# Gated attention and MLP on one core: one weight load moved ahead of two attention loads, its splits ahead of an evacuation

## The chip, the cores and the metric

The kernel runs on 1 core of one Trainium2 chip. The metric is the device time of one execution in microseconds, the median over several runs; lower is better. The work is spread over the core's engines: TensorE (PE in the profile, its weight loads PEld), VectorE (DVE), ScalarE (ACT), GpSimd (POOL), and SyncE (SP), which here issues every DMA.

## What is computed

For a sequence of 2048 tokens of width D = 448 the kernel computes two branches on the same x and mixes them by a gate of one number per token:

```python
x = A_x
g = _sigmoid((x * gate_w).sum(-1, keepdims=True))
# branch A: 16 heads of 28; each token attends to 8 positions, every second one back from itself
qkv = x @ wqkv
logits = einsum("bhsd,bhswd->bhsw", q, kg) * scale      # masked where the position is below 0
a = (softmax(logits) applied to vg) @ wo
# branch B: F = 1792
h = relu(x @ w1 + b1) ** 2
b = h @ w2 + b2
return g * a + (1 - g) * b
```

All inputs and the output are float32. Each product is made of three passes over a high and a low part of both operands (high·high, high·low, low·high), so every operand is first split: a copy that rounds to the high part, and a subtraction that leaves the low part.

## The kernel before

**Stages.** Tokens come in four chunks of 512 (chunk order in the MLP: 3, 0, 1, 2). First TensorE makes q, k and v of chunks 0, 1 and 2; ScalarE copies the results out of PSUM (the evacuations, L243) into staging tiles, and SP stores these to DRAM (`q_d`, `k_d`, `v_d`). Then comes chunk 3 in two calls of `qkv_two`, two token tiles each. The second call has the first two pairs of MLP hidden tiles (`mlp_one`, `mlp_two`) put in between its own products. After that comes the MLP for all chunks, `h` products (x by w1) and `b` products (h by w2) in turn, with the output projection `a` worked in near the end.

**Attention** runs beside all this on GpSimd and VectorE, in eight units: GpSimd multiplies q by k (L561, eight pieces of a unit), VectorE sums the products (L562), then softmax, then GpSimd multiplies by v (L568). A unit's q and k are loaded by SP (L532 and L533) into one buffer each, so the loads for the second unit wait until GpSimd has finished the first unit's eight pieces.

**What sets the order.** Nothing is scheduled at run time: each engine runs its instructions in the order in which the Python code emits them. A model clock, `clock["pe"]`, is moved on by `advance` with each group of matmuls; `when(t, fn, ...)` and `at(dt, fn)` put a piece of work on a list, and `advance` emits what is due. So the numbers in the `when` table decide where in an engine's queue a piece stands; they are not times on the chip. If a piece waits for data, everything behind it on that engine waits too.

**The weights w2.** `w2_piece(i0, n, t, gap)` loads n row blocks of w2 (128x448 each) into one buffer of the two-buffer pool `rawp` (L792) and puts one split per block at t, t + gap and so on. The first load holds blocks 0 to 3 (896 KB), the second blocks 4 to 6 (672 KB). A split (`split_copied`) is a ScalarE copy to the high part `w2ah` (L745), a second ScalarE copy of the raw block into one PSUM bank, `copy` (L746), and a VectorE subtraction to the low part `w2al` (L751). All seven splits share the one `copy` bank, so a second copy waits for the subtraction before it. The first load's buffer is the one that the third w1 load had: its last readers are ScalarE's copies of that load.

**PSUM banks.** There are eight, four of tag "m" and four of tag "b". In the second `qkv_two` the accumulators q0, q1 and k1 hold three "m" banks, and the first hidden pair (h0, h1) takes the fourth and then q0's bank, once ScalarE has evacuated q0. A hidden pair's products come in two halves, between which the two tiles change sides of the array; ScalarE marks the change by a touch of the weights (L814, `h_turn`), which waits for the first half and for which the second half waits. In the same way a VectorE memset (L212, `turned` and `turn`) marks the change for q, k and v.

**The biases.** `biases()` issues two DMAs: b1 into `b1t` (part of tile `b1z`, L1024), used by the ReLU on ScalarE (L867), and b2 spread over all partitions into `b2t` (L1025). Until then `b2t` serves as the staging tile of a v evacuation, whose store is the DMA `v_d<-b2t` (L230).

Of the kernel before, what the change touches and what calls it, by code (L numbers as in the profile page):

```python
# [57 lines left out]
def gated_mix_kernel(ctx: ExitStack, tc: tile.TileContext, xT, wqkv, w1, w2, wo, b1, b2, out):  # L58
# [868 lines left out]
    def when(t, fn, *args):  # L927
        later.append((t, lambda: fn(*args)))
# [129 lines left out]
    when(66000.0, w1_piece, 3, 83700.0, 900.0)  # L1058
    for j in range(2):
        when(63700.0 + j * 2000.0, x_copy, 3, j)  # L1060
    when(76700.0, biases)
    when(83700.0, w2_piece, 0, 4, 93400.0, 1350.0)
    when(87400.0, w2_piece, 4, 3, 99000.0, 1350.0)

    pair = {}
# [441 lines left out]
```

## Time and profile before

| | us |
|---|---|
| median of 3 runs | 413.45 (413.06 to 413.98) |
| the profiled execution: time, and its span | 414.4, 412.6 |
| PE busy in the span | 405.5 (98%) |
| DVE, ACT, POOL busy | 288.2, 219.3, 267.4 |
| PE idle in the stretch 100 to 115 | 2.22 of 15 |
| granted TensorE clock | 1.0 |

The profile shows one execution, which took 0.95 us more than the median; its span leaves out 1.8 us of that execution's time. Busy time is a sum over stages; what a change of order is worth is read from the stage in which it stands, from what each engine waited for there. In rows of a timeline the first number is the start and the second the duration, both in us from the span's start, and a bracket at the end gives the idle time of the engine just before that row and what ended it.

### The profile page before, as it was taken

The page shows a single profiled execution, that of the slowest core. Times are in us where ns is not written, and L with a number is a line of the kernel's source. Part 1 is how long each engine was busy: PE and PEld are TensorE (multiplying, and loading weights), DVE is VectorE, ACT ScalarE, POOL GpSimd, SP SyncE. Part 2 cuts the span into 40 slices and gives each one's busy share as a digit, 9 for nine tenths or more (in the row PEclk, how much of TensorE's full clock was granted, in tenths as well). Part 3 has the DMA queues.
Part 4 walks back from the last instruction along what each step waited for, and adds up shares of the span by engine and source line. Part 5 has one row for each costly group of instructions (what it writes and reads, how often), then busy time and mean ns, then how long its engine had stood idle before and what let it go on. Part 6 is the DMA issues. An engine that isn't in the chain of part 4 may idle for free.

```text
span 412.6 us, 9369 instructions
## 1 busy us (share of the span) xinstructions
PE 405.5 (98%) x3799; PEld 361.8 (88%) x3799; DVE 288.2 (70%) x480; ACT 219.3 (53%) x498; POOL 267.4 (65%) x167
## 2 busy tenths in 40 slices
PE   8999999999999999999999999999999999999996
PEld 7999999998878888888888888988898888888996
DVE  3997884674768667687755898779676677784344
ACT  4858577372875565444565435444643254346640
POOL 0000001864999999979999799898989978950000
PEclk9999999999999999999999999999999999999999
DMA  7999999949463605654023648855146630049404
GB/s 217 353 359 262 361 374 259 371 132 348 166 210 127 207 4 179 207 186 152 8 78 106 193 140 247 248 153 157 39 153 197 220 129 0 25 126 180 120 3 178
DMA packets 67548, 73.99 MB, mean 179 GB/s; under 512 B 34544, under 2 KB 59824, under 8 KB 67376
## 3 DMA queue, kind: packets, MB, share of 16 engines
q1 hardware_dynamic: 67504, 73.39, 56.1%
q8 instruction: 29, 0.48, 0.5%
q14 instruction: 15, 0.12, 0.1%
HBM read 45.94 MB, written 28.25 MB: 180 GB/s over the span
## 4 chain that ended last, share of the span: by engine, by line
PE 92%; DMA 3%; ACT 2%; DVE 1%; issue 0%; SPq 0%
PE b L202 33%; PE h L202 31%; PE a L202 7%; PE qkv L202 7%; PE v L344 4%; PE x L344 3%; DMA w2raw<-w 2%; PE z L344 2%; PE qkv L291 2%; PE y L344 1%; PE w L344 1%; DMA xraw<-xT 1%; PE a L1279 1%; ACT st L243 1%; ACT copy L746 1%; DVE w2al L751 1%
## 5 line engine op out<-in xcount | busy, mean ns | idle before, releaser
L561 POOL TENSOR_TENSOR qk<-q,k 128x896 f32<-128x896 f32 x64 | 134.6, 2138 | 86.6 <-DMA k<-k_d 79.0
L568 POOL TENSOR_TENSOR av<-lg,v 128x896 f32<-128x896 f32 x64 | 118.9, 1976 | 4.7 <-DVE lg L562 4.5
L866 DVE TENSOR_TENSOR h<-h,h 128x512 fp32r<-128x512 f32 x56 | 38.5, 688 | 58.2 <-ACT h L869 57.7
L562 DVE TENSOR_REDUCE lg<-qk 128x32 f32<-128x896 f32 x64 | 67.1, 1074 | 0.0
L576 DVE TENSOR_REDUCE o<-av 128x112 f32<-128x896 f32 x64 | 66.6, 1070 | 0.3 <-POOL av L568 0.3
L202 PE MATMUL b<-w2ah,h 64*128 64x448 f32 x448 | 66.3, 359 | 0.0
L202 PE MATMUL b<-w2bh,h 64*128 64x448 f32 x448 | 66.1, 359 | 0.0
L867 ACT ACTIVATE h<-h,b1z 128x512 f32<-128x512 f32 x56 | 36.7, 655 | 42.1 <-PE h L202 42.1
L202 PEld LDWEIGHTS b<-w2bh,h 64*128 64x128 f32 x448 | 42.1, 184 | 3.6
L202 PEld LDWEIGHTS b<-w2ah,h 64*128 64x128 f32 x448 | 42.0, 184 | 3.7
L202 PE MATMUL b<-w2bl,h 64*128 64x448 f32 x224 | 40.6, 358 | 0.0
L202 PE MATMUL b<-w2al,h 64*128 64x448 f32 x224 | 40.5, 358 | 0.0
L202 PE MATMUL qkv<-wqh,x 64*128 64x448 f32 (+1 forms) x240 | 36.6, 361 | 0.0
L868 ACT ACTIVATE h<-h 128x512 fp32r<-128x512 f32 x56 | 33.5, 598 | 1.7
L869 ACT ACTIVATE h<-h 128x512 f32<-128x512 f32 x56 | 33.3, 594 | 0.0
L814 ACT ACTIVATE h<-h 128x4 fp32r<-128x4 f32 (+1 forms) x35 | 7.2, 207 | 43.4 <-PE b L202 41.1
L202 PEld LDWEIGHTS qkv<-wqh,x 64*128 64x128 f32 x240 | 23.7, 185 | 1.7
L202 PE MATMUL qkv<-wql,x 64*128 64x448 f32 (+1 forms) x120 | 22.8, 361 | 0.0
L202 PEld LDWEIGHTS b<-w2bl,h 64*128 64x128 f32 x224 | 21.1, 184 | 1.9
L202 PEld LDWEIGHTS b<-w2al,h 64*128 64x128 f32 x224 | 21.0, 184 | 1.9
L202 PE MATMUL h<-x,w1ah 64*128 64x512 f32 x84 | 17.4, 389 | 0.7 <-ACT w1ah L814 0.7
L243 ACT ACTIVATE st<-qkv 128x448 f32<-128x448 f32 x24 | 12.3, 542 | 7.4 <-DVE xraw L969 3.2
(280 smaller groups left out, 899.2 us busy)
## 6 DMA issues: line engine op xcount, KB each, us to landing
k<-k_d SPq DMA_DIRECT2D x8, 840.0 KB, 6.6
v<-v_d SPq DMA_DIRECT2D x8, 840.0 KB, 4.7
x_d<-x SPq DMA_DIRECT2D x12, 512.0 KB, 8.2
q_d<-st SPq DMA_DIRECT2D x8, 448.0 KB, 7.0
k_d<-st SPq DMA_DIRECT2D x8, 448.0 KB, 7.9
w1raw<-w SPq DMA_DIRECT2D x4, 896.0 KB, 14.1
q<-q_d SPq DMA_DIRECT2D x8, 448.0 KB, 4.1
o_d<-o SPq DMA_DIRECT2D x16, 224.0 KB, 2.2
```

What stands on the lines that cost most here:

```text
L202: nc.tensor.matmul(acc.pt[:, :acc.n], a[rows], w[rows], start=acc.todo == acc.all, stop=acc.todo == 1)
L243: nc.scalar.activation(st[:, :, t % 2], heads(pt), AF.Copy)
L291: nc.tensor.matmul(acc.pt[:, :D], a, w, start=k == j == 0, stop=False)
L344: nc.tensor.matmul(self.pt[:, :self.n], a, w, start=new, stop=True, skip_group_check=True)
L561: nc.gpsimd.tensor_mul(pr, q[:, s:s + 1].to_broadcast([P, W, C]), k[:, s:s + W])
L562: pending.append(lambda: nc.vector.tensor_reduce(lg[:, s], pr.rearrange("p w (h d) -> p w h d", h=HG), axis=AX.X, op=ALU.add))
L568: nc.gpsimd.tensor_mul(pr.rearrange("p (h d) w -> p w h d", h=HG), lg[:, s][:, :, :, None].to_broadcast([P, W, HG, DH]), v[:, s:s + W].rea ...
L576: nc.vector.tensor_reduce(o[:, g * C:(g + 1) * C], pr, axis=AX.X, op=ALU.add)
L866: nc.vector.tensor_sub(hl, pt, f32(hh))
L867: ops += [lambda pt=pt, r=r: nc.scalar.activation(pt, pt, AF.Relu, bias=b1t[:, f + r:f + r + 1]), lambda pt=pt, hh=hh: nc.scalar.activatio ...
L868: lambda pt=pt, hh=hh: nc.scalar.activation(hh, pt, AF.Square),
L869: lambda pt=pt, r=r, low=low: (nc.scalar.activation(pt, pt, AF.Square), at(delays[r], low))]
```

## The change

It alters three numbers and the order of two lines in the `when` table:

```diff
-    when(76700.0, biases)
-    when(83700.0, w2_piece, 0, 4, 93400.0, 1350.0)
+    when(85000.0, biases)
+    when(81000.0, w2_piece, 0, 4, 90000.0, 1350.0)
     when(87400.0, w2_piece, 4, 3, 99000.0, 1350.0)
```

No instruction is added or taken away. What moves is shown below at three places.

SP's queue, in the stretch after the last v stores of chunk 2 (`w2raw_1455` and `w2raw_1413` are the first w2 load, `w2raw_1550` the second; `q_1442` and `k_1443` are the second attention unit's; the `st` tiles are chunk 3's staged q, k and v):

```order
 L230 DMA v_d<-b2t 128x4x112
+L792 DMA w2raw_1413<-w 128x4x448
+L532 DMA q_1442<-q_d 128x896
+L533 DMA k_1443<-k_d 128x1680
+L235 DMA q_d<-st_0_0_1426 128x4x224
+L235 DMA k_d<-st_1_1_1428 128x4x224
 L1024 DMA b1z<-b 128x14
 L1025 DMA b2t<-b 128x448
-L532 DMA q_1442<-q_d 128x896
-L533 DMA k_1443<-k_d 128x1680
-L792 DMA w2raw_1455<-w 128x4x448
-L235 DMA q_d<-st_0_0_1426 128x4x224
```

The w2 load now stands first, right behind the store of `b2t`, and the two bias loads stand behind q, k and two stores.

ScalarE's queue around the evacuations of the second `qkv_two` (`qkv_2_0` is q0, `qkv_3_1` is k1), before:

```order
L243 ACTIVATE st_2_0_1618<-qkv_2_0_1490 128x4x112
L243 ACTIVATE st_3_1_1620<-qkv_3_1_1493 128x4x112
L745 ACTIVATE w2ah<-w2raw_1455 128x448
L746 ACTIVATE copy_1496<-w2raw_1455 128x448
L745 ACTIVATE w2ah<-w2raw_1455 128x448
L746 ACTIVATE copy_1496<-w2raw_1455 128x448
L814 ACTIVATE w1ah<-w1ah 128x2
```

And the same place now:

```order
L745 ACTIVATE w2ah<-w2raw_1413 128x448
L746 ACTIVATE copy_1496<-w2raw_1413 128x448
L745 ACTIVATE w2ah<-w2raw_1413 128x448
L746 ACTIVATE copy_1496<-w2raw_1413 128x448
L243 ACTIVATE st_2_0_1624<-qkv_2_0_1490 128x4x112
L243 ACTIVATE st_3_1_1626<-qkv_3_1_1493 128x4x112
L814 ACTIVATE w1ah<-w1ah 128x2
```

Two splits stand ahead of these rows in both; before, the other two of the first load came behind the evacuation of q0 and k1, and now all four come ahead of it.

VectorE's queue, the low parts against the memsets (`qkv_3_0` is k0, `qkv_2_1` is q1) and attention's sums (the change, one piece of the difference):

```order
+L751 TENSOR_TENSOR w2al<-copy_1496,w2ah 128x448
 L212 MEMSET qkv_3_0_1491 1x1
 L212 MEMSET qkv_2_1_1492 1x1
+L751 TENSOR_TENSOR w2al<-copy_1496,w2ah 128x448 x2
 L562 TENSOR_REDUCE lg_1184<-qk_7_1415 128x32
 L212 MEMSET qkv_2_2_1494 1x1
 L212 MEMSET qkv_3_2_1495 1x1
```

Three of the four low parts now stand ahead of the memsets of v and of the first unit's last sum; one of them stands ahead of the memsets of q1 and k0. The fourth comes behind the second unit's first sum.

## The prediction, made before the changed kernel was run

> **What bounds the kernel now.** I read the page's busy line first, then TensorE's own list of waits, then its windows, and went from the two waits found there to the engines behind them.
>
> ```profile
> PE 405.5 (98%) x3799; PEld 361.8 (88%) x3799; DVE 288.2 (70%) x480; ACT 219.3 (53%) x498; POOL 267.4 (65%) x167
> PE h L202 <- ACT st L243: 1.5, 1, 1.5
> PE h L202 <- ACT w1ah L814: 0.7, 1, 0.7
> 116.80:380.00 263.20, 263.20 (x2492) 232.93 (x2490) 190.69 (x247) 132.14 (x293) 231.78 (x136) 1.00 0.46 143
> ```
>
> TensorE is the bound: from 116.8 to 380 it has no idle time (the second number equals the first; the granted clock, third from the end, is 1.00). Outside the start and the end it waits for others twice, both times for ScalarE, and both waits lie in the stretch that the change rearranges. TensorE's timeline there:
>
> ```profile
> 101.81 0.39 PE L202 MATMUL h<-x,w17h 64*128 64x512 f32 x1
> 103.71 0.50 PE L202 MATMUL h<-x,w17h 64*128 64x512 f32 x1 [1.51 <-ACT st L243]
> ...
> 109.61 0.61 PE L202 MATMUL h<-x,w17h 64*128 64x512 f32 x2
> ...
> 112.33 0.36 PE L202 MATMUL qkv<-wqh,x 64*128 64x450 f32 x1
> ...
> 113.58 0.36 PE L202 MATMUL qkv<-wqh,x 64*128 64x450 f32 x1
> 114.64 0.50 PE L202 MATMUL h<-x,w1ah 64*128 64x512 f32 x2 [0.71 <-ACT w1ah L814]
> ```
>
> The idle numbers (1.51 and 0.71) understate the loss: in the first gap one half of the array had a matmul and the other none. I take the loss from the cadence. Twelve pairs of 512 columns take 2.72 (109.61 to 112.33), so nine take 2.04; six pairs of 448 or 450 columns take 1.24 (112.33 to 113.58). Undisturbed from 101.81: hidden pair 2.72, six pairs of q, k, v 1.24, second half 2.04, next hidden pair 2.72, six pairs 1.24, in all 9.96. TensorE could be at the row of 114.64 by 101.81 + 9.96 = 111.77. The two waits cost **2.87 us**, and no more than that is to be had here.
>
> ScalarE shows why:
>
> ```profile
> 86.61 0.55 ACT L746 ACTIVATE copy<-w1raw 128x448 f32<-128x448 f32 x1 [0.81 <-DVE w17l L751]
> ...
> 92.70 1.25 ACT L130 ACTIVATE w17h<-w1raw 64x64 fp32r<-64x64 f32 x4
> 100.94 0.58 ACT L745 ACTIVATE w2ah<-w2raw 128x448 fp32r<-128x448 f32 x1 [6.99 <-DMA w2raw<-w]
> 101.43 0.53 ACT L746 ACTIVATE copy<-w2raw 128x448 f32<-128x448 f32 x1
> ...
> 102.64 0.55 ACT L746 ACTIVATE copy<-w2raw 128x448 f32<-128x448 f32 x1 [0.19 <-DVE w2al L751]
> 103.13 1.07 ACT L243 ACTIVATE st<-qkv 128x448 f32<-128x448 f32 x2
> ...
> 106.75 0.21 ACT L814 ACTIVATE w1ah<-w1ah 128x2 fp32r<-128x2 f32 x1 [0.41 <-PE h L202]
> ...
> 111.83 0.64 ACT L867 ACTIVATE h<-h,b1z 128x512 f32<-128x512 f32 x1
> ...
> 114.39 0.20 ACT L814 ACTIVATE w1ah<-w1ah 128x2 fp32r<-128x2 f32 x1
> ```
>
> It stands still for 6.99 us, from the end of the w17h splits (93.95) until the first w2 load lands (100.94). Then two splits run at 1.21 us each (101.43 to 102.64), and the evacuation of q0, whose bank h1 needs, starts only at 103.13. Its data were there earlier: q0's products end six pairs before 101.81, at 100.57, plus about 0.16 (a 0.36 us matmul outlasts its 0.20 slot by that). The backlog also reaches the ReLU (111.83), and behind it the touch (114.39) that the second gap waits for. Why the load is late is on SP:
>
> ```profile
> 83.49 1.05 SPq L230 DMA_DIRECT2D v_d<-b2t  x1
> ...
> 90.06 0.35 SPq L1025 DMA_DIRECT2D b2t<-b  x1
> 90.50 0.38 SPq L532 DMA_DIRECT2D q<-q_d  x1
> 90.93 0.42 SPq L533 DMA_DIRECT2D k<-k_d  x1
> 91.45 0.39 SPq L792 DMA_DIRECT2D w2raw<-w  x1
> ...
> 97.92 1.29 SPq L792 DMA_DIRECT2D w2raw<-w  x1
> SPq L1025 <- DMA v_d<-b2t: 4.2, 1, 4.2
> 87.00:88.00 1.00, 1.00 (x14) 0.93 (x12) 1.00 (x4) 0.16 (x1) 1.00 (x2) 1.00 0.09 24
> 100.00:101.00 1.00, 1.00 (x12) 0.94 (x10) 0.00 (x0) 0.06 (x1) 1.00 (x2) 1.00 1.09 375
> 105.00:106.00 1.00, 1.00 (x12) 0.84 (x10) 0.87 (x2) 0.80 (x3) 1.00 (x2) 1.00 0.34 125
> ```
>
> The b2 load overwrites the tile that `v_d<-b2t` still reads, so SP is held for 4.2 us, to 90.06, with q, k and w2 behind it, while the DMA engines are nearly idle (0.09 busy, 24 GB/s at 87; 375 GB/s at 100).
>
> **The change part by part.**
>
> *The w2 load (one DMA) moved ahead of the biases, q and k.* It needs its buffer, which ScalarE reads last at 86.61 + 0.55 = 87.16. So it is issued at about 87.2, 4.2 us sooner. How long it then takes no row shows; the nearest, and the ones that bound it, are these landing times (the last number, from issue):
>
> ```profile
> w2raw<-w SPq DMA_DIRECT2D x1, 896.0 KB, 9.5
> k<-k_d SPq DMA_DIRECT2D x1, 840.0 KB, 7.7
> q<-q_d SPq DMA_DIRECT2D x1, 448.0 KB, 5.7
> q_d<-st SPq DMA_DIRECT2D x1, 448.0 KB, 10.4
> k<-k_d SPq DMA_DIRECT2D x1, 840.0 KB, 4.8
> w1raw<-w SPq DMA_DIRECT2D x2, 896.0 KB, 14.1
> ```
>
> The first four were issued at 90.5 to 91.9 behind one another. The k load of 4.8 is the first unit's, with little in flight; w1raw's 14.1 is of a stretch where the engines were full throughout. At 87.2 they are nearly idle, so I take the short end: 4.8 x 896/840 = 5.1, landing at 92.3 (bounds 92.3 and 101.3). ScalarE reaches the first split at 93.95, so its 6.99 us wait goes.
>
> *All four splits ahead of the q0 evacuation.* Two more are there, 2.42 us of ScalarE. Four at 1.21 from 93.95 end at 98.8, before the evacuation's data at 100.73: they lie inside the old 6.99 us of idle time and cost nothing. If the load lands after about 96, that cover is gone (rival 2). The evacuation then runs 100.73 to 101.3, before h1's slot (101.81 + 0.23). **First gap: gone.**
>
> *Low parts ahead of memsets on VectorE.*
>
> ```profile
> 96.61 0.14 DVE L212 MEMSET qkv<- 1x1 f32 x2 [1.16 <-PE qkv L202]
> 78.62 10.47 POOL L561 TENSOR_TENSOR qk<-q,k 128x896 f32<-128x896 f32 x5 [1.58 <-DMA v_d<-st]
> 98.72 6.25 POOL L561 TENSOR_TENSOR qk<-q,k 128x896 f32<-128x896 f32 x3 [9.63 <-DMA k<-k_d]
> 105.67 2.07 DVE L562 TENSOR_REDUCE lg<-qk 128x32 f32<-128x896 f32 x2
> ```
>
> The first low part is ready at about 95.5 and is over before TensorE lets the q1/k0 memsets run (96.61); these are needed at 100.57. Cost nothing, with 4 us of slack.
>
> *The q and k loads* (two DMAs) now follow the w2 load. They wait for GpSimd's last piece of the first unit (78.62 + 10.47 = 89.09) instead of SP's 90.06: issued 1.35 us sooner, with 896 KB ahead of them and the 224 KB of b2 no longer. The w2 bytes move largely in the idle time before 91, so I take a landing of 96.5 against 98.72 before. Bounds: 89.6 + 4.8 = 94.4, and 99.7 (rival 1).
>
> *The biases* (two DMAs) move past five others. Their wait is over at 90.06, before SP reaches them. b1 is first read by the ReLU, at 108.8 below; even a landing of 10.4 after an issue at 93 leaves 5 us. Behind them on SP are the v store and the second w2 load. That load was issued at 97.92 and its bytes were through before 106 (0.34 busy, then quiet); 896 KB of the traffic now leaves earlier, which at 375 GB/s is 2.4 us, so I take a landing by 103.5; its first split is due at 104.85.
>
> *The second gap.* ScalarE's chain: the touch at 104.53 + 0.19 = 104.74 (hidden pair ends 101.81 + 2.72); 0.11 to the first copy of the next split, 0.47 and 0.48 for its two copies, 0.86 for the two evacuations, 0.47, 1.21, 0.49 for the last two splits: ReLU at 108.8. From ReLU to TensorE's start took 114.64 - 111.83 = 2.81, so 111.65 against the 111.77 at which TensorE is ready. The second gap closes with 0.1 to spare, so I leave 0.1 of the 2.87 unclaimed.
>
> **Sum:** 2.8 us off TensorE's path. Behind it TensorE has no wait until 380 and the order of all engines is unaltered; the end keeps its own waits. Against the profiled execution: 414.4 - 2.8 = 411.6 (span 409.8). That execution was 0.95 above the median, so on the median 413.45 - 2.8 = 410.65, say **410.7**.
>
> **The rivals.**
>
> 1. *The keys land late, and half the gain goes.* The keys feed GpSimd; VectorE sums its products in an order in which the fifth and sixth low parts stand behind the second unit's third sum. The old landing, 98.72, puts that sum's end at 98.72 + 6.25 + 1.04 (half of 2.07) = 106.0, about when the fifth low part is wanted (105.8); each us beyond 98.8 delays the touch by as much. Counted from before: issue 1.35 sooner, 896 KB more ahead (2.4 us at 375 GB/s), would give 98.6 + 2.4 - 1.35 = 99.7: 0.9 lost, **411.6**. For it: the four landings above (96.2, 98.6, 100.9, 102.3) came in order of issue. Against it: the idle engines at 87. The Trainium skill ("DMA: Bandwidth & Descriptors", Queues, rings and completion order) says that on each DMA engine descriptors of one queue are consumed in ring order, so that what stands ahead is always paid; by that rule the time is this rival's unless the weights are through before the keys are issued. The trace's order of landing agrees.
>
> 2. *Slower: the w2 load lands late all the same.* With the splits ahead of the evacuation on an in-order engine, a late load now blocks more. Before, a landing at 100.94 let the evacuation start at 103.13, behind two splits; behind four it ends 2.19 + 2.42 + 0.54 = 5.15 after the landing X. Beyond X = 96.9 TensorE waits for it, and since the row of 114.64 follows h1's start by 9.96 - 0.23 = 9.73, it breaks even at X = 99.8. At w1raw's 14.1 from 87.2, X = 101.3: h1 at 106.45, the row of 114.64 at 116.2, time **415.0**. Against it: the full engines behind that 14.1 are absent at 87.
>
> 3. *The second w2 load lands late,* because the biases are issued ahead of it. At the old end of its bytes, 106, the chain from 104.85 moves by 1.15: **411.8**.
>
> 4. *Nothing measurable:* the load is held on SP until 91.4 by something that the trace does not show (the old row at 91.45 has no visible reason to be that late but its neighbours) and lands near 98.5, so that h1 starts about as before, and the keys behind it land near 101 and take most of the second gap back: **413.2**.
>
> **How the numbers follow.** Chances: forecast 0.70, rival 1 0.12, rival 3 0.07, rival 4 0.05, rival 2 0.06. A run of this kernel scatters from 413.06 to 413.98, so about 0.2% (0.8 us) is what can be told from no change. Forecast and rivals 1 and 3 are faster by more than that, save a rival 1 with keys later than 100.8 (0.03): faster 0.86, same 0.08, slower 0.06. The range runs from the whole 2.87 and a scatter of 0.4 (410.2) to rivals 1 and 3 with as much scatter (412.2), and leaves out 0.15.
>
> **What would show it.** Right: w2 issued near 87.2 and landed before 94, no DMA wait on ScalarE before its first w2 copy; the q0 evacuation near 100.7; TensorE without an idle row from 101 to 114, the row of 114.64 near 111.8. Wrong: a ScalarE wait on w2raw that lasts beyond 96, a VectorE wait on GpSimd's products ahead of a low part, or keys that land after 98.8.

## The result and the profile after

| | kernel before | changed kernel | changed / before |
|---|---|---|---|
| first comparison, median of 6 runs each | 413.70 us (413.06 to 414.03) | 411.34 us (411.06 to 411.82) | 0.9946, 95% 0.9933 to 0.9959 |
| repeated in a later set of runs, 20 and 8 runs | 412.53 us (411.82 to 413.36) | 411.23 us (410.9 to 412.9) | 0.9975, 95% 0.9963 to 0.9988 |
| profiled execution: time, span | 414.4, 412.6 us | 411.63, 409.9 us | |

The change makes the kernel faster, by 0.54% in the first comparison and by 0.25% in the second. 410.7 us had been predicted, with 411.6 for the profiled execution and 409.8 for its span. The changed kernel takes the same in both; what differs is the kernel before. That difference is the subject of half the experiments.

The page of the changed kernel, its busy line, followed by the shares of the engines in its chain of work:

```profile
PE 404.7 (99%) x3799; PEld 362.8 (89%) x3799; DVE 288.2 (70%) x480; ACT 219.4 (54%) x498; POOL 267.5 (65%) x167
...
PE 97%; DMA 1%; SPq 0%; DVE 0%; ACT 0%; issue 0%
```

TensorE's own waits in the changed kernel (total, times, longest), the whole list, and then two of its windows:

```profile
PE warm L879 <- DVE b1z L877: 1.2, 1, 1.2
PE qkv L291 <- ACT x L911: 0.8, 1, 0.8
100.00:115.00 15.00, 15.00 (x140) 13.99 (x140) 10.93 (x15) 10.25 (x24) 14.92 (x11) 1.00 0.30 103
115.00:380.00 265.00, 265.00 (x2510) 234.57 (x2508) 191.43 (x249) 132.37 (x295) 231.35 (x135) 1.00 0.47 143
```

Both waits for ScalarE are off the list; what is left belongs to the start. In the stretch of the change TensorE is busy for 15.00 of 15.00 us. Its timeline there, with no idle number in any row:

```profile
102.03 0.42 PE L202 MATMUL h<-x,w17h 64*128 64x512 f32 x2
...
112.02 0.42 PE L202 MATMUL h<-x,w1ah 64*128 64x512 f32 x2
...
114.10 0.37 PE L202 MATMUL b<-w2ah,h 64*128 64x448 f32 x2
```

From 102.03 to 112.02 it takes 9.99, where the prediction worked out 9.96 for an undisturbed TensorE. (This execution was 0.22 us behind the earlier one before the change bears on it: chunk 3's q, k, v start at 79.03 against 78.81. So its times are to be read 0.22 later than the predicted ones.)

SyncE of the changed kernel, then ScalarE:

```profile
83.31 1.02 SPq L230 DMA_DIRECT2D v_d<-b2t  x1
86.98 0.38 SPq L792 DMA_DIRECT2D w2raw<-w  x1
88.86 0.33 SPq L532 DMA_DIRECT2D q<-q_d  x1
89.25 0.42 SPq L533 DMA_DIRECT2D k<-k_d  x1
...
92.71 0.96 SPq L1025 DMA_DIRECT2D b2t<-b  x1
...
95.12 0.78 SPq L792 DMA_DIRECT2D w2raw<-w  x1
```

```profile
86.41 0.55 ACT L746 ACTIVATE copy<-w1raw 128x448 f32<-128x448 f32 x1 [0.80 <-DVE w17l L751]
...
92.92 1.25 ACT L130 ACTIVATE w17h<-w1raw 64x64 fp32r<-64x64 f32 x4
94.20 0.58 ACT L745 ACTIVATE w2ah<-w2raw 128x448 fp32r<-128x448 f32 x1
...
98.81 0.55 ACT L746 ACTIVATE copy<-w2raw 128x448 f32<-128x448 f32 x1 [0.19 <-DVE w2al L751]
101.36 0.98 ACT L243 ACTIVATE st<-qkv 128x448 f32<-128x448 f32 x2 [2.00 <-PE qkv L202]
...
109.10 0.64 ACT L867 ACTIVATE h<-h,b1z 128x512 f32<-128x512 f32 x1
...
111.66 0.20 ACT L814 ACTIVATE w1ah<-w1ah 128x2 fp32r<-128x2 f32 x1
```

The w2 load is issued the moment ScalarE has read its buffer (86.41 + 0.55 = 86.96), 4.5 us sooner than before. The first w2 split follows the w17h splits directly, with no wait for a DMA, and all four are over at 99.36, before the evacuation has its data. That evacuation now waits for TensorE (2.00), where TensorE used to wait for it. The last four rows end the second gap: the touch at 111.66 is over at 111.86, and the hidden row at 112.02 has nothing to wait for.

VectorE, GpSimd and the DMA engines of the changed kernel:

```profile
95.55 0.64 DVE L751 TENSOR_TENSOR w2al<-copy,w2ah 128x448 fp32r<-128x448 f32 x1
...
96.82 0.14 DVE L212 MEMSET qkv<- 1x1 f32 x2 [0.64 <-PE qkv L202]
96.36 6.31 POOL L561 TENSOR_TENSOR qk<-q,k 128x896 f32<-128x896 f32 x3 [7.53 <-DMA k<-k_d]
87.00:88.00 1.00, 1.00 (x14) 0.94 (x12) 1.00 (x5) 0.00 (x0) 1.00 (x1) 1.00 0.20 49
90.00:91.00 1.00, 1.00 (x14) 0.93 (x12) 0.41 (x1) 0.89 (x3) 0.00 (x0) 1.00 1.04 401
102.00:103.00 1.00, 1.00 (x12) 0.91 (x12) 0.61 (x2) 0.34 (x1) 1.00 (x2) 1.00 0.07 21
```

The low part stands in VectorE's idle time ahead of the memset, which still waits for TensorE. The second keys land at 96.36. The DMA engines, at 49 GB/s at 87, are at 401 GB/s at 90, three us after the issue of the weights, and by 102 nearly nothing moves any more (21 GB/s).

### The profile page after: what moved, and what is told of

Its sections match the earlier page's. It is cut to its first block, busy times and chain, and to the rows that moved or that the text cites. A ratio compares the mean times of both kernels' runs of the same rounds, so it can differ in the third digit from the quotient of the medians.

```text
span 409.9 us, 9374 instructions
## 1 busy us (share of the span) xinstructions
PE 404.7 (99%) x3799; PEld 362.8 (89%) x3799; DVE 288.2 (70%) x480; ACT 219.4 (54%) x498; POOL 267.5 (65%) x167
## 4 chain that ended last, share of the span: by engine, by line
PE 97%; DMA 1%; SPq 0%; DVE 0%; ACT 0%; issue 0%
PE b L202 33%; PE h L202 33%; PE qkv L202 11%; PE a L202 7%; PE v L344 4%; PE x L344 3%; PE z L344 2%; PE qkv L291 1%; DMA xraw<-xT 1%; PE y L344 1%; PE w L344 1%; PE a L1279 1%; PE last L1279 0%; SPq L891 0%; SPq L886 0%; DVE bt L1158 0%
## 5 line engine op out<-in xcount | busy, mean ns | idle before, releaser
L866 DVE TENSOR_TENSOR h<-h,h 128x512 fp32r<-128x512 f32 x56 | 38.5, 689 | 58.5 <-ACT h L869 58.1
L202 PEld LDWEIGHTS qkv<-wqh,x 64*128 64x128 f32 x240 | 22.8, 185 | 1.5
L202 PE MATMUL qkv<-wql,x 64*128 64x448 f32 (+1 forms) x120 | 21.9, 361 | 0.0
L202 PE MATMUL h<-x,w1ah 64*128 64x512 f32 x84 | 16.5, 387 | 0.0
```

The source lines that it names most:

```text
L202: nc.tensor.matmul(acc.pt[:, :acc.n], a[rows], w[rows], start=acc.todo == acc.all, stop=acc.todo == 1)
L866: nc.vector.tensor_sub(hl, pt, f32(hh))
```

## The experiments

**How they are read.** A few tenths of a per cent are close to the scatter of the runs, so I read each profile also by one stretch: from the start of chunk 3's q, k, v on TensorE to the first row that reads w2 (`b<-w2ah`). Undisturbed it takes 35.06, as in the second profile of the changed kernel. What it takes beyond that is what a kernel loses to waits there.

| kernel | q, k, v start | first `b` row | stretch | lost | b2 load / first w2 load issued |
|---|---|---|---|---|---|
| before, first profile | 78.81 | 116.81 | 38.00 | 2.94 | 90.06 / 91.45 |
| before, second | 78.02 | 114.24 | 36.22 | 1.16 | 87.68 / 89.07 |
| before, third | 78.39 | 114.66 | 36.27 | 1.21 | 87.38 / 89.04 |
| before, fourth | 78.67 | 114.80 | 36.13 | 1.07 | 87.34 / 88.73 |
| changed, first profile | 79.03 | 114.10 | 35.07 | 0.01 | 92.71 / 86.98 |
| changed, second | 78.69 | 113.75 | 35.06 | 0 | 92.27 / 86.59 |
| biases alone, first | 78.17 | 113.78 | 35.61 | 0.55 | 91.77 / 87.73 |
| biases alone, second | 78.59 | 114.23 | 35.64 | 0.58 | 92.05 / 88.15 |
| loads moved, old splits | 78.52 | 114.12 | 35.60 | 0.54 | 91.99 / 86.42 |
| splits alone | 78.67 | 118.20 | 39.53 | 4.47 | 87.57 / 88.96 |
| w2 and splits, old biases | 78.10 | 113.84 | 35.74 | 0.68 | 87.87 / 88.31 |
| keys behind v | 78.29 | 118.81 | 40.52 | 5.46 | 91.89 / 86.19 |
| keys last | 78.64 | 121.13 | 42.49 | 7.43 | 92.24 / 86.55 |

The first four experiments take the change apart and share one chip and one set of runs of the kernel before (412.45 us, 411.6 to 413.44, 29 runs). The recorded expectations call them e1 to e4, in this order, and the two experiments with later keys e5 and e6.

### The biases' loads alone

```diff
-    when(76700.0, biases)
+    when(85000.0, biases)
```

> Only the biases' loads are moved (w2's load stays behind q and k, two splits stay behind the evacuation of q0). Theory (only the landing time counts: the splits in the old order hold the evacuation no more once the load lands before about 98.5): q, k and w2 are issued at 89 to 90, w2 lands near 96.5, both TensorE waits are gone, 411.3 against 413.7 before, as with the whole change. Rival (the w2 load has to stand ahead of the keys): w2 lands at 98.5 or later, less than half of the gain, 412.6 or more.

Measured: 412.34 us (411.31 to 413.02, 12 runs), ratio 0.9999, 95% 0.9989 to 1.0008. That isn't the 411.3 expected. The profiled execution was the fastest of the twelve. ScalarE in it, and the row of TensorE that still waits:

```profile
97.33 0.58 ACT L745 ACTIVATE w2ah<-w2raw 128x448 fp32r<-128x448 f32 x1 [4.01 <-DMA w2raw<-w]
...
100.18 0.98 ACT L243 ACTIVATE st<-qkv 128x448 f32<-128x448 f32 x2 [0.49 <-PE qkv L202]
...
105.27 0.55 ACT L746 ACTIVATE copy<-w2raw 128x448 f32<-128x448 f32 x1 [0.45 <-DVE w2al L751]
111.61 0.50 PE L202 MATMUL h<-x,w1ah 64*128 64x512 f32 x2 [0.29 <-ACT w1ah L814]
```

The load still stands behind the keys and lands at 97.3. The evacuation is in time, so there is no first gap. But the second pair of splits comes behind the evacuation, and on VectorE the fourth low part (104.62 to 105.23) stands behind two of attention's sums: the copy of the fifth split waits 0.45 us for it, the ReLU comes later by about as much, and 0.55 us of the second gap stays. Neither the theory (both waits gone) nor its rival (w2 at 98.5 or later) describes this.

### The loads moved, the splits where they were

```diff
-    when(76700.0, biases)
-    when(83700.0, w2_piece, 0, 4, 93400.0, 1350.0)
+    when(85000.0, biases)
+    when(81000.0, w2_piece, 0, 4, 93400.0, 1350.0)
```

> Both moves of loads, but the splits where they were (two ahead of q0's evacuation, two behind). Theory: the load lands before 94, the two later splits run between the evacuation (102.3) and the touch (105.0) in ScalarE's idle time, nothing lost, 411.3. Rival (the splits' place is part of the gain, since two splits of 1.2 us stand ahead of the touch): the first gap is closed, the second is not, 412.0 to 412.5.

Measured: 411.87 us (411.45 to 413.01, 11 runs), ratio 0.9992, 95% 0.9983 to 1.0002. ScalarE and the same row of TensorE:

```profile
99.48 0.55 ACT L746 ACTIVATE copy<-w2raw 128x448 f32<-128x448 f32 x1 [4.27 <-DVE w2al L751]
100.52 0.98 ACT L243 ACTIVATE st<-qkv 128x448 f32<-128x448 f32 x2 [0.49 <-PE qkv L202]
111.94 0.50 PE L202 MATMUL h<-x,w1ah 64*128 64x512 f32 x2 [0.28 <-ACT w1ah L814]
```

No row waits for the DMA any more, yet ScalarE stands still for 4.27 us all the same: the low part that it waits for stands on VectorE behind the memsets of v, which wait for TensorE. That wait itself delays nothing, since the evacuation still has to wait for TensorE (0.49). What costs is the same wait as with the biases alone, 0.45 us of the fifth split's copy for the fourth low part: 0.54 us of the second gap stays. So the theory, that nothing is lost, fell, and the rival's account holds, though the time is below its 412.0. An early load alone isn't enough; the place of the splits in both queues is part of the gain.

### The splits alone

```diff
-    when(83700.0, w2_piece, 0, 4, 93400.0, 1350.0)
+    when(83700.0, w2_piece, 0, 4, 90000.0, 1350.0)
```

> Only the splits are moved; both loads stay as before. Theory (the prediction's rival 2: a late load behind an in-order engine): w2 lands at 100.9, the evacuation ends 5.15 later at 106.1, h1 starts there instead of at 103.7, the next half follows by 9.73 at 115.8 instead of 114.6, so slower by 1.2: 414.9. Rival (ScalarE does the same work either way, the order is neutral): 413.7.

Measured: 415.07 us (413.64 to 416.91, 6 runs), ratio 1.0062, 95% 1.0039 to 1.0085. ScalarE, TensorE, and TensorE's granted clock (third from the end) in two windows:

```profile
99.25 0.58 ACT L745 ACTIVATE w2ah<-w2raw 128x448 fp32r<-128x448 f32 x1 [5.43 <-DMA w2raw<-w]
...
103.91 0.96 ACT L243 ACTIVATE st<-qkv 128x448 f32<-128x448 f32 x2
101.05 0.47 PE L202 MATMUL qkv<-wqh,x 64*128 64x448 f32 x2 [0.42 <-DVE qkv L212]
...
104.49 0.53 PE L202 MATMUL h<-x,w17h 64*128 64x512 f32 x1 [1.73 <-ACT st L243]
104.00:106.00 2.00, 1.51 (x8) 1.29 (x10) 2.00 (x6) 0.87 (x2) 1.53 (x2) 0.71 0.03 9
106.00:108.00 2.00, 2.00 (x12) 1.56 (x12) 2.00 (x3) 0.00 (x0) 2.00 (x2) 0.50 0.00 0
```

This is the mechanism of rival 2. With four splits ahead of it the evacuation is held by a late load: the load landed at 99.25, and the evacuation's first half ends at 103.91 + 0.54 = 104.45, 5.20 later, where the prediction had 5.15. The sooner splits are a loss unless the load is early. A memset that now stands behind a low part holds TensorE too (0.42); the longer wait behind it hides that. The second hidden tile starts 2.59 late by these waits (104.49 against 78.67 + 23.23, the undisturbed distance). The rest of the 4.47 is for the most part not a wait: the granted clock falls to 0.50, which costs an estimated 1.7. It didn't fall in every execution: two of the six runs kept a clock of 1.0 and took 413.64 and 413.94, the other four, at 0.995 to 0.996, took 415.02 to 416.91. So the expected 414.9 is met by luck. The load came 1.7 sooner than expected, and the lower clock made up for it.

### The w2 load and its splits, the biases where they were

```diff
-    when(83700.0, w2_piece, 0, 4, 93400.0, 1350.0)
+    when(81000.0, w2_piece, 0, 4, 90000.0, 1350.0)
```

> w2's load and splits moved, the biases left where they were, so that SP is still held by b2 until about 90. Theory: w2 lands near 97 and the keys near 100.9; the first wait is 0.3 to 0.5, and the late keys hold the fifth and sixth low parts, so the second gap is about 2; of the gain 0.5 to 0.9 is left, 412.8 to 413.2. Rival (moving w2 ahead is the gain, the biases do not matter): 411.3.

Measured: 412.89 us (411.92 to 413.87, 12 runs), ratio 1.0009, 95% 0.9997 to 1.0021. ScalarE, GpSimd and TensorE:

```profile
95.36 0.58 ACT L745 ACTIVATE w2ah<-w2raw 128x448 fp32r<-128x448 f32 x1 [2.11 <-DMA w2raw<-w]
98.63 6.30 POOL L561 TENSOR_TENSOR qk<-q,k 128x896 f32<-128x896 f32 x3 [11.73 <-DMA k<-k_d]
111.67 0.50 PE L202 MATMUL h<-x,w1ah 64*128 64x512 f32 x2 [0.40 <-ACT w1ah L814]
```

Issued at 88.31 behind the b2 load, the weights land at 95.4, soon enough for the first gap, and the keys at 98.6. Rival 1 names 98.8 as the limit for the keys, for a first h row at 101.81; here that row is at 101.10, which puts the limit at 98.1. The keys are 0.54 late and the row of 111.67 is 0.61 late (101.10 + 9.96 = 111.06). 0.68 us of the stretch stays lost.

The time is what was expected, but not for the reasons given: the weights and the keys landed 1.6 and 2.3 us sooner than the theory says, and beside these runs of the kernel before there is no gain. Behind the stretch this profile has another wait of 0.5 that no other kernel here shows (for a hidden part of VectorE, L866). I did not follow it further.

So none of the four combinations gives a gain in its runs that can be told from no change; the whole change does. The w2 load alone, and the biases with the splits, were not run. By the profiles each of the three combinations that lose less than the kernel before still loses at least 0.5 us, and that the whole change is better than the loads without the splits rests on the profiles (0 against 0.54 lost), since the intervals of the two overlap.

### The second keys later

To test rival 1 as a rule, two kernels issue the second q and k loads of the changed kernel later, behind the v store, and behind that and the second w2 load. They differ in the delay alone (2500 and 4000):

```diff
-                if i not in qk:
+                if i not in qk and i != 1:
...
-                        qk[1] = att_load_qk(*units[1])
+                        at(2500.0, lambda: qk.update({1: att_load_qk(*units[1])}))
```

> The changed kernel with the second unit's q and k loads issued later, behind the biases and the v store, ahead of the second w2 load. Theory (rival 1's mechanism: keys that land after about 98.8 delay the touch by as much, through VectorE's sums ahead of the fifth low part): the keys land near 100.5, TensorE waits for the touch for 1.5 to 1.9, slower than the whole change by that much. Rival (attention has slack there): no wait, same time as the whole change.

> As e5, with the keys behind the second w2 load too. Theory: they land near 102.3, the wait for the touch is 3.3 to 3.7, the loss against the whole change 3.3 to 3.7, one us for each us of landing. Rival (the keys matter, but VectorE or ScalarE have slack after the first us): the loss is as in e5 or below 2.5.

These ran together with the second comparison. Behind v: 416.44 us (415.51 to 417.88, 6 runs), ratio 1.0105, 95% 1.0088 to 1.0121. Last: 418.99 us (418.76 to 419.2, 4 runs), ratio 1.0162, 95% 1.0148 to 1.0175. GpSimd, ScalarE and TensorE of the first, then GpSimd and TensorE of the second:

```profile
102.02 6.31 POOL L561 TENSOR_TENSOR qk<-q,k 128x896 f32<-128x896 f32 x3 [15.10 <-DMA k<-k_d]
110.53 0.55 ACT L746 ACTIVATE copy<-w2raw 128x448 f32<-128x448 f32 x1 [2.78 <-DVE w2al L751]
115.06 0.68 PE L202 MATMUL h<-x,w1ah 64*128 64x512 f32 x2 [3.59 <-ACT w1ah L814]
```

```profile
104.13 6.26 POOL L561 TENSOR_TENSOR qk<-q,k 128x896 f32<-128x896 f32 x3 [16.85 <-DMA k<-k_d]
117.12 0.80 PE L202 MATMUL h<-x,w1ah 64*128 64x512 f32 x2 [3.89 <-ACT w1ah L814]
```

The rule of rival 1 holds: each us of the keys beyond 98.8 delays the row behind the second gap (115.06 and 117.12 here) by as much. The first h row is at 101.29 and 101.64 in these profiles, 0.52 and 0.17 before the 101.81 on which 98.8 rests. Behind v, the row is late by 115.06 - (101.29 + 9.96) = 3.81 and the keys by 102.02 - (98.8 - 0.52) = 3.74; last, 117.12 - (101.64 + 9.96) = 5.52 and 104.13 - (98.8 - 0.17) = 5.50. The changed kernel, with its keys at 96.4, is 2.7 us on the safe side (its limit is 98.8 + 0.22). The times are 5.2 and 7.8 us above the changed kernel's, where 1.5 to 1.9 and 3.3 to 3.7 were expected, for two reasons: the keys landed 1.5 and 1.8 later than expected, and the loss is larger than the wait, because the granted clock fell in both. TensorE's windows, first behind v, then last:

```profile
114.00:116.00 2.00, 0.94 (x6) 0.76 (x8) 1.97 (x5) 2.00 (x7) 2.00 (x2) 0.80 0.00 0
116.00:118.00 2.00, 2.00 (x12) 1.63 (x10) 1.79 (x3) 1.00 (x4) 2.00 (x2) 0.50 0.06 20
```

```profile
116.00:118.00 2.00, 0.88 (x4) 0.79 (x6) 1.97 (x5) 2.00 (x7) 2.00 (x2) 0.50 0.00 0
118.00:120.00 2.00, 2.00 (x12) 1.53 (x12) 1.80 (x3) 1.05 (x5) 2.00 (x2) 0.50 0.03 10
120.00:122.00 2.00, 2.00 (x14) 1.64 (x12) 0.00 (x0) 0.63 (x1) 2.00 (x2) 0.50 1.02 307
```

### Both kernels again, and the kernel before twice more

> The whole change again, beside the kernel before on the chip of these runs, because in the runs of e1 to e4 the kernel before took 412.45 and not 413.7. Theory (what the change takes away is a loss of the kernel before that varies with the landing of the store of b2t, which held SP to 90.06 in the first profile and to 87.6 and 87.9 in e3 and e4): the changed kernel is as fast as before this, 411.0 to 411.4, and the gain is smaller here, 1.0 to 1.5. Rival (the gain is a fixed 2.4, and the whole chip was faster by 1.2): 410.0 to 410.2.

> The kernel before, profiled here. Theory: b2's load is issued at 87.6 to 88, w2 lands near 99.3, q0's evacuation ends near 102.0 and both TensorE waits together cost 1.3 to 1.8 instead of 2.9; ratio to itself 1.000. Rival (fixed loss): SP held to about 90 and TensorE waits of 1.5 and 0.7 as in the first profile.

The changed kernel: 411.23 us, ratio 0.9975 as in the table at the top. The kernel before against itself: 412.53 (411.77 to 413.72, 12 runs), ratio 1.0004, 95% 0.9994 to 1.0014. Two more profiles of the kernel before, and a second one of the biases alone, were taken later on another chip, one run each:

> The kernel before once more, unchanged, for a third profile of it. Theory: its time is the start of chunk 3's q, k, v on TensorE, plus the stretch from there to the first row that reads w2 (35.06 undisturbed), plus 297.55 (the value in seven earlier profiles, within 0.15); the stretch loses 1.2 to 2.9 here and more the later the b2 load and with it the first w2 load leave SP (90.06 and 91.45 gave 2.9; 87.68 and 89.07 gave 1.2). Rival: the loss in the stretch is the same in every execution and the scatter of the times lies elsewhere; then the stretch is 36.2 or 38.0 whatever SP does, and the sum misses by more than 0.5.

> A fourth profile of the kernel before, with the same expectation: time = start of chunk 3's q, k, v + stretch + 297.55 within 0.2, a loss of 1.2 to 2.9 in the stretch that goes with the issue of the first w2 load (89.1 to 91.5).

> The kernel with the biases' loads alone moved, for a second profile: its median of 412.3 says that a usual execution loses about 1 us more than the one profiled first (411.3, 0.55 lost). Theory: the first w2 load, still behind the second keys, lands later than the 97.3 of that profile, at 98 to 100, and the stretch loses 0.8 to 2. Rival: the stretch loses 0.5 again and the time above 411.3 comes from a later start of chunk 3 or from behind the stretch.

They took 412.45, 412.64 and 412.12 us. The second profile of the kernel before, SyncE, ScalarE and TensorE:

```profile
87.68 0.35 SPq L1025 DMA_DIRECT2D b2t<-b  x1
89.07 0.38 SPq L792 DMA_DIRECT2D w2raw<-w  x1
98.36 0.58 ACT L745 ACTIVATE w2ah<-w2raw 128x448 fp32r<-128x448 f32 x1 [5.19 <-DMA w2raw<-w]
...
100.55 1.05 ACT L243 ACTIVATE st<-qkv 128x448 f32<-128x448 f32 x2
...
105.71 0.55 ACT L746 ACTIVATE copy<-w2raw 128x448 f32<-128x448 f32 x1 [0.85 <-DVE w2al L751]
112.05 0.50 PE L202 MATMUL h<-x,w1ah 64*128 64x512 f32 x2 [0.68 <-ACT w1ah L814]
```

The store of `b2t` was through at 87.7 here, not at 90.06. The load therefore lands 2.6 us sooner than in the first profile, the evacuation starts at 100.55 instead of 103.13, and the first gap isn't there at all. The third and fourth profiles read the same: b2 issued at 87.4 and 87.3, only the second gap left, 1.21 and 1.07 us lost. So the first profile, with 2.94, showed a loss that three others of the same kernel don't have, and the theory that the loss goes with the issue of these loads fits the four. Three of them are alike, though, and one alone is late. The second lost a little less than expected (1.16 and not 1.3 to 1.8), since its load landed at 98.4 and not at 99.3.

The second gap isn't a matter of the load alone, however. The fifth split's copy (105.71) waits 0.85 us for VectorE, where the fourth low part stands behind two of attention's sums. The first profile has the same wait (0.88, at 108.31). The loss of the kernel before therefore has two parts:

| | before, four profiles in order | changed, both |
|---|---|---|
| first hidden row to the touch that ends the first half | 4.94, 3.17, 3.22, 3.05 | 2.99 |
| from that touch to the ReLU | 5.08, 5.06, 5.06, 5.07 | 4.08 |

The first part goes with the load: 1.95 us are lost in the first profile, 0.06 to 0.23 in the others. The second part, 1.0 us, is the same in all four. Where the load lands sooner still and the splits keep their places (the biases alone, the loads moved) it is 4.65, so 0.57 us of it belongs to the order of the queues.

The sum with 297.55 came out 0.24 and 0.29 too low for the third and fourth, a little outside the 0.2 I had given it. It is less steady than the expectation says: time less the first `b` row is 297.72 in the changed kernel's second profile, and 298.07 and 298.78 with the keys last and with the old biases.

For the biases alone my theory fell and its rival held: the load landed at 97.5 and not at 98 to 100, the stretch lost 0.58 as in its first profile, and the time above 411.3 came from a start of chunk 3 at 78.59 instead of 78.17 and from 0.3 behind the stretch. By the profiles this part gains about 0.6 (0.57 lost against 1.1 to 1.2), or 0.14%; the interval of its runs reaches only 0.11%, so that the runs neither show this gain nor quite allow it.

## Why the prediction was right, point by point

- *The w2 load at 87.2, landed at 92.3:* issued at 86.98. Where exactly it landed no row says, since nobody waits for it any more: it was there before 94.20.
- *Four splits in ScalarE's idle time, over before the evacuation:* over at 99.36; the evacuation started at 101.36, where 100.73 + 0.22 was predicted. The 0.16 that I had put for the end of q0's products was 0.4 too little, with no effect.
- *Low parts ahead of the memsets cost nothing:* right for the one that the trace can show, 95.55 + 0.64 before 96.82.
- *The keys at 96.5:* 96.36. Rival 1 didn't come to pass, but the experiments show its limit and its price to be as worked out, one us for one us. They also agree with the rule quoted beside it from the Trainium skill ("DMA: Bandwidth & Descriptors", Queues, rings and completion order): keys issued at 89.25 behind the weights landed at 96.4, and issued at 89.30 behind b2 and the weights at 98.6. (The 102.0 and 104.1 of the later keys show mostly their later issue, at 94.12 and 95.81.)
- *The second w2 load in time, by 103.5 (rival 3):* issued at 95.12, and from 102 the DMA engines moved only 21 GB/s.
- *Rival 4, something unseen that holds the load until 91.4:* there was nothing of the kind; the load left 0.02 after its buffer was free.
- *Rival 2, late weights:* shown as a mechanism by the splits alone; in the change the load is early.
- *The second gap as ScalarE's backlog behind the late load:* only in part. Three profiles of the kernel before have an earlier load, no first gap, and still 1.0 us of this loss, because the fourth low part stands behind two sums on VectorE. With the loads moved and the old splits 0.57 of it is left, and it takes the splits' new places on VectorE to remove that. The predicted chain has no wait for VectorE there, as measured, but gives no reason for that.
- *The second gap closes with 0.1 to spare:* the touch ended at 111.86 and the row started at 112.02, without an idle number, and the stretch had 35.07 and 35.06 in two executions.
- *The sum of 2.8:* right to 0.1 for the profile from which it was worked out (span 412.6 to 409.9, time 414.4 to 411.63), too large for the medians (2.36 in the first comparison, 1.3 in the second). The term that was mis-sized is the loss of the kernel before, "the two waits cost 2.87", taken from one execution. I noted that this execution was 0.95 above the median but took the whole 2.87 off the median as well. In three other executions of it the loss was 1.07 to 1.21, because the store on which the biases, the keys and the weights waited was through 2.4 to 2.7 us sooner, so that next to nothing was lost to the first gap. The 1.3 of the second comparison agrees with that. The 2.36 of the first lies between the two; whether each of its executions lost about that much, or some 2.9 and some 1.1, isn't shown, since only one was profiled in it. That the measured gain came near to 2.8 is therefore in part luck of the first comparison: beside the later runs of the kernel before it is less than half of that. The mechanism for the changed kernel was right in both.

Apart from two waits at the start of the kernel, TensorE has no wait left in either profile of the changed kernel, so a better order of these loads has nothing more to win in this stretch.

## What to carry to other kernels

A wait that ends with a transfer has a length of its own in each execution: here the late load cost 1.95 us in one and 0.06 to 0.23 in three others of the same program, while another 1.0 us, for the most part from the order of the queues, was there each time. Before the whole of a gap is claimed, ask how the profiled execution stands to the median, and how much of the gap is left if the transfer lands two us sooner. When work is put earlier on an in-order engine, move what it waits for first, and look at both queues that it uses: here the sooner splits alone lost 0.6%, the sooner loads without the splits gained nothing that the runs could show, and of what was run only the load, the splits and the biases together left TensorE without a wait.

## What the runs showed of the hardware

**A wait can cost more than its length.** After waits of 3.59 and 3.89 us TensorE came back at a granted clock of 0.50. Windows of 0.5 us put the fall and the return of the clock at 115.2 and 118.6 behind v, at 115.4 and 122.3 with the keys last, and at 104.8 and 108.2 with the splits alone. At half the clock, the part of this time in which TensorE had work is an estimated 1.7, 2.6 and 1.7 us lost beside the wait: the stretch behind v lost 5.46 for a row that was 3.81 late. The Trainium skill ("TensorE: Matmul & The Clock Gate", Part 1: The HAM clock gate) gives half rate after an idle window of about 3.4 us and calls the window free-running; the run behind v agrees. But with the keys last the clock fell only 2.2 us after the last matmul had ended (113.23), and with the splits alone it fell to 0.50 after a wait of only 1.73, preceded by one of 0.42 shortly before, while the 1.51 in the first profile of the kernel before left it at 1.00. There the measurement decides: a wait below 3.4 us isn't safe. Nor does each such wait cost the clock: one of the six runs behind v kept it at 1.0 (415.51 us), as did two of the six with the splits alone.

**The end of one store can hold SyncE while little moves, for a time that differs between executions.** In the first profile the store of `b2t`, issued at 83.49, held SyncE until 90.06, while the DMA engines moved 24 GB/s at 87 and 7 at 89. In the three later profiles the same wait was over at 87.3 to 87.7. In two of these the store took nearly as long (6.4 and 6.0 us from its issue, against 6.6) but was issued at 81.3 and 81.4; in the third it was issued at 82.96 and took 4.4. Why the issue and the length of the store differ isn't shown; the order of the program is the same. Through the loads behind it, this one store made the stretch 1.7 to 1.9 us longer in one profile of the kernel before than in the others.
